# First head pair laid out by compute engines in a written order, expert matrices loaded in pieces, value products and sums placed by tables

## The chip, the core and the metric

One core of a Trainium2 chip runs the program. The metric is the time of one execution on the device in microseconds. Three runs of the kernel before gave 1154.0, 1154.58 and 1159.22 us; their median is 1154.58 us.

## What is computed

Three blocks follow each other. The first is attention over 4 batches of 8 heads (1152 keys of 64 numbers) whose queries are pooled by two; the second sends its output through four causal experts of which each token takes two; the third mixes tokens by two low-rank matrices and ends in an MLP.

```python
# attention: q, k, v are 4 x 8 x 1152 x 64
q_pool = q.reshape(B, H, S // 2, 2, D).mean(axis=3)
scores = scale * np.matmul(q_pool, k.transpose(0, 1, 3, 2))
scores = scores - np.max(scores, axis=-1, keepdims=True)
attn = np.exp(scores)
attn = attn / (np.sum(attn, axis=-1, keepdims=True) + 1e-09)
x = np.matmul(attn, v)              # to 4 x 576 x 512
# experts: per expert q, k, v = x @ wq[e], x @ wk[e], x @ wv[e]; causal softmax,
# @ wo[e], times the token's weight for this expert if it is one of its best two
# tokens and MLP
u = x + (x.transpose(0, 2, 1) @ U @ V).transpose(0, 2, 1)
out = u + np.maximum(u @ w_ch1, 0.0) @ w_ch2
```

## The kernel before

**Pairs and units.** The 32 heads are worked through as 16 pairs. `prep(i)` makes pair `i` ready, `unit(i, u)` is one of its 18 units: a half `h` of the 576 queries against one of nine key tiles `kt`. A unit has two scores (`score(0)` and `score(1)`, one for each head of the pair, in the score tile `st`), the exponentials of them on ACT into `pt`, a running sum of these on POOL (`acc`), and the products with the values (`pv`, two matmuls of half the columns each). After the ninth unit of a half come `post_a` (column sums on TensorE), `post_r` and `post_b` (reciprocal and scaling on DVE). A score is the sum of two matmuls, `q1`·`s1` (line 576) and `q2`·`s2` (line 577): numbers are kept as a high and a low part in fp32r, and one row of `q2` holds minus the maximum of each query's scores.

**What a pair needs first.** `pool_q` adds neighbouring queries into `qp` on DVE (line 495). `tr_q` transposes them on TensorE (511), ACT takes the high part `qh` out of PSUM (517), DVE the low part `ql` (520), and two DMAs for each `tr_q` lay `qh` as blocks into `BD` (522). `tr_k` does the same with the keys: `kn` (361) and `klo` (364). `lay` issues 12 DMAs that copy `qh`, `ql`, `kn` and `klo` into the tiles `q1a`, `q2a`, `s1a`, `s2a` and their twins `q1b` to `s2b`, whose other half of the partitions POOL has filled with constants (351 to 354). The maximum of each query is found by 27 matmuls `mxs` of `BD` with `kn` (543), each reduced by DVE (545) out of one of three PSUM buffers `ms`. `fin` turns the maxima into a row (406, `nm` 408) and sends it by DMA into `q2a` and `q2b` (411); it is called for a block of five and a block of four query tiles, for the first and the second half of the queries.

**Order.** In the attention stage TensorE, DVE and ACT run in the order in which the code is written. `attend` counts two steps for each unit, 36 for a pair. In each step it calls one score, then what `side` holds for that step; tables (`Q_AT`, `K_AT`, `M_AT`, ...) give the steps of `prep(i)` relative to the first step of pair `i`. After every third unit come the value products of three units, the last of which is the unit before the last one scored; `post_a` follows one such group after the half's last product. Pair 0 is prepared ahead of this, by `run_all`, in an order that the scheduler may change, and so are those steps of pair 1 that lie before step 0.

**Loads.** All DMAs are issued by SP in one queue. `expert_weights` loads the expert matrices `wq`, `wk`, `wv`, `wo` and the token matrices U and V one after the other into two halves of a staging tile `stg` (280 to 324), all DMAs of a matrix in one step, and cuts each into a high and a low part, three pieces for a pair of heads (`WC_AT`). U and V are 64-bit numbers, which six DVE instructions turn into 32 bits (248 to 253).

Of the kernel before, what the change touches and what calls it, by code (L numbers as in the profile page):

```python
# [19 lines left out]
GROUP = 3  # L20
POOL_AT, LQ_AT, LK_AT, V_AT = -13, -48, -24, 6
Q_AT = [-7, -1]
K_AT = [-1, 5, 11]
LAY_AT = 13
M_AT = [3, 4, 6, 7, 8, 9, 10, 12, 13, 14, 15, 16, 18, 19, 20, 21, 22, 24, 25, 26, 27, 30, 31, 32, 33, 36, 37]
F_AT = [23, 41]

WL_AT, WC_AT = 20, [17, 23, 35]
# [28 lines left out]
def attend(units, side):  # L57

    n, done, ended, later = len(units), 0, [], {}

    def run(t):
# [5 lines left out]
    def sums(t):  # L69
        nonlocal ended  # L70
        for x in ended:
            x[0]()
            later.setdefault(t + 1, []).append(x[1])
            later.setdefault(t + 4, []).append(x[2])
        ended = []

    for u in range(n):
        for a in range(2):
            units[u][0](a)
            run(2 * u + a)  # L80
        if u % GROUP == GROUP - 1 or u == n - 1:
            last = n if u == n - 1 else u - 1
            sums(2 * u + 1)
            for x in units[done:last]:
                x[1]()
                if x[2]:
                    ended.append(x[2])
            done = last
    sums(2 * n - 1)
    t = 2 * n  # L90
    while side or later:
        run(t)
        t += 1
# [39 lines left out]
def kernel(  # L133
# [36 lines left out]
    nc.vector.tensor_copy(identb, ident)  # L170
    negid = cst.tile([P, 64], F32, name="negid")
    for r in (0, 64):
        nc.vector.tensor_scalar(negid[r:r + 64], ident[r:r + 64, r:r + 64], -1.0, None, op0=ALU.mult)
# [13 lines left out]
    nc.vector.tensor_copy(mask_t, mtmp)  # L187
# [7 lines left out]
    nc.vector.tensor_copy(mask_m[:, T - 64:], mtmp2)  # L195
# [60 lines left out]
    def expert_weights():  # L256
# [17 lines left out]
        def heads(x, w, dst):  # L274
            t = part(x, NC, dst[0].shape[-1])

            def load():
                nc.vector.memset(t[:1, 0, ::HD], 0.0)
                for e in range(E):
                    nc.sync.dma_start(t[:, :, e * HD:(e + 1) * HD], w[e].rearrange("(c p) d -> p c d", p=P))  # L280
                if t.shape[-1] > EW:
                    nc.sync.dma_start(t[:, :, EW:], w_gate.rearrange("(c p) e -> p c e", p=P))

            return load, pieces(t, *dst, 4)
# [638 lines left out]
    with tc.manual_schedule(engines=by_hand):  # L923
        attend(units, side)
# [215 lines left out]
```

## Time and profile before

| | us |
|---|---|
| median of three runs | 1154.58 |
| span of the profiled execution | 1150.9 |
| TensorE busy in it | 1112.5 |
| DVE, POOL, ACT busy | 753.4, 496.2, 459.2 |
| its attention stage | about 32 to 498 |

The span goes from the first to the last instruction; the 3.7 us between it and the median are not in the profile. A matmul's end is modelled, so where matmuls follow each other the distance of their starts tells more than their length. A time in brackets behind a row is idle time of that engine just before it, with what ended it.

### The profile page before, as it was taken

How to read it: one execution, taken by the hardware profiler on the slowest of the kernel's cores; microseconds unless marked ns; L12 is line 12 of the kernel's file. 1: busy time of each engine (PE TensorE's matmuls, PEld its weight loads, DVE VectorE, ACT ScalarE, POOL GpSimd, SP SyncE). 2: the span in 40 equal slices, each digit the busy share in tenths (PEclk: the TensorE clock that was granted, in tenths of full speed). 3: DMA queues.
4: the chain of work that ended last, by engine and by line, in shares of the span. 5: the costliest groups of instructions: out<-in, count | busy, mean ns of one | idle time of the engine just before them, and what ended most of it. 6: DMA issues, size and time to landing. Idle time of an engine off the chain costs nothing.

```text
span 1150.9 us, 19012 instructions
## 1 busy us (share of the span) xinstructions
PE 1112.5 (97%) x6748; PEld 900.0 (78%) x6748; DVE 753.4 (65%) x1613; ACT 459.2 (40%) x1160; POOL 496.2 (43%) x473
## 2 busy tenths in 40 slices
PE   5999999999999999899999998999999999999998
PEld 3777777777777777678777876688899999999997
DVE  6677888888888777566848489946734661663222
ACT  1555666655555555543444535512211111111111
POOL 4688989888788888764324243200000000000000
PEclk9999999999999999999999999999999999999999
DMA  9788787777777764111213134341110220110111
GB/s 223 163 180 195 163 205 170 171 166 166 175 176 166 165 146 118 32 38 46 53 32 94 25 101 166 112 151 55 56 38 19 60 69 1 55 55 1 56 56 55
DMA packets 116958, 120.02 MB, mean 104 GB/s; under 512 B 71680, under 2 KB 88064, under 8 KB 116864
## 3 DMA queue, kind: packets, MB, share of 16 engines
q1 hardware_dynamic: 116864, 118.82, 41.8%
q8 instruction: 53, 0.87, 0.3%
q14 instruction: 41, 0.34, 0.1%
HBM read 52.65 MB, written 9.44 MB: 54 GB/s over the span
## 4 chain that ended last, share of the span: by engine, by line
PE 83%; DVE 12%; ACT 2%; DMA 1%; POOL 1%; issue 1%; SPq 0%; ACTq 0%; POOLq 0%
PE ms L1046 17%; PE o L1057 17%; PE pv L596 11%; PE ms L692 8%; PE st L576 8%; PE ms L543 6%; PE st L577 6%; PE pv L843 2%; DVE mp L545 2%; PE ms L603 2%; DVE ms L767 1%; PE ms L502 1%; DMA bd<-qh 1%; PE st L818 1%; DVE xl L232 1%
## 5 line engine op out<-in xcount | busy, mean ns | idle before, releaser
L588 POOL TENSOR_TENSOR acc<-acc,pt 128x576 f32<-128x576 f32 x224 | 326.5, 1458 | 61.4 <-ACT pt L578 46.8
L578 ACT ACTIVATE pt<-st 128x288 f32<-128x288 f32 x576 | 219.0, 410 | 185.1 <-PE st L577 157.9
L545 DVE TENSOR_REDUCE mp<-ms 128x1 f32<-128x384 f32 x432 | 213.0, 545 | 56.3 <-PE ms L543 55.7
L1046 PE MATMUL ms<-uh,w 128*128 128x384 f32 x768 | 214.7, 340 | 0.9 <-DVE ul L232 0.7
L1057 PE MATMUL o<-w,hh 128*128 128x512 f32 x576 | 180.9, 395 | 0.0
L1050 DVE SCALAR_TENSOR_TENSOR hl<-ms,hh 128x384 fp32r<-128x384 f32 x96 | 53.5, 557 | 186.9 <-ACT hh L1049 186.5
L543 PE MATMUL ms<-kn,bd 128*128 128x384 f32 x432 | 151.7, 361 | 11.9 <-DMA bd<-qh 9.2
L596 PE MATMUL pv<-pt,vr 128*64 128x288 f32 x1152 | 159.6, 413 | 0.0
L1049 ACT ACTIVATE hh<-ms 128x384 fp32r<-128x384 f32 x96 | 47.2, 492 | 270.9 <-PE ms L1046 270.9
L1046 PEld LDWEIGHTS ms<-uh,w 128*128 128x128 f32 x768 | 140.9, 188 | 6.3 <-DVE ul L232 0.9
L1046 PE MATMUL ms<-ul,w 128*128 128x384 f32 x384 | 129.9, 338 | 0.7 <-DVE ul L232 0.7
L1057 PEld LDWEIGHTS o<-w,hh 128*128 128x128 f32 x576 | 107.0, 188 | 17.8 <-issue 0.4
L596 PEld LDWEIGHTS pv<-pt,vr 128*64 128x64 f32 x1152 | 77.1, 137 | 55.5 <-issue 11.2
L1057 PE MATMUL o<-w,hl 128*128 128x512 f32 x288 | 113.6, 394 | 0.0
L543 PEld LDWEIGHTS ms<-kn,bd 128*128 128x128 f32 x432 | 84.0, 195 | 18.6 <-DVE mp L545 7.0
L576 PE MATMUL st<-q1a,s1a 128*128 128x288 f32 x288 | 97.4, 338 | 0.7 <-ACT pt L578 0.7
L576 PEld LDWEIGHTS st<-q1a,s1a 128*128 128x128 f32 x288 | 54.3, 189 | 45.7 <-issue 40.7
L576 PE MATMUL st<-q1b,s1b 128*128 128x288 f32 x288 | 86.2, 299 | 0.4 <-ACT pt L578 0.3
L577 PE MATMUL st<-q2a,s2a 128*128 128x288 f32 x288 | 85.2, 296 | 0.0
L577 PE MATMUL st<-q2b,s2b 128*128 128x288 f32 x288 | 85.0, 295 | 0.0
L1046 PEld LDWEIGHTS ms<-ul,w 128*128 128x128 f32 x384 | 72.2, 188 | 5.1 <-DVE ul L232 1.7
L835 POOL TENSOR_TENSOR acc<-acc,pt 128x576 f32<-128x576 f32 (+4 forms) x48 | 45.4, 945 | 67.1 <-ACT pt L826 65.8
(172 smaller groups left out, 1834.1 us busy)
## 6 DMA issues: line engine op xcount, KB each, us to landing
raw<-in_moe_w_ch_dram SPq DMA_DIRECT2D x32, 512.0 KB
qr<-in_q_dram SPq DMA_DIRECT2D x16, 576.0 KB
vr<-in_v_dram SPq DMA_DIRECT2D x16, 576.0 KB
s1a<-kn SPq DMA_DIRECT2D x32, 288.0 KB
s1b<-kn SPq DMA_DIRECT2D x32, 288.0 KB
kr<-in_k_dram SPq DMA_DIRECT2D x30, 288.0 KB
s2a<-klo SPq DMA_DIRECT2D x16, 288.0 KB
s2b<-klo SPq DMA_DIRECT2D x16, 288.0 KB
```

Of the source, the lines that this page charges most:

```text
L543: nc.tensor.matmul(ps[:, :384], BD[i % 2][:, t, :], KN[i % 2][:, c * 384:c * 384 + 384], start=True, stop=True)
L545: nc.vector.tensor_reduce(st["mp"][:, t, c:c + 1], ps[:, :384], axis=X, op=ALU.max)
L576: nc.tensor.matmul(ps[:, :HT], pr.S1[a][:, ks], pr.Q1[a][:, qs], start=True, stop=False)
L577: nc.tensor.matmul(ps[:, :HT], pr.S2[a][:, ks], pr.Q2[a][:, qs], start=False, stop=True)
L578: nc.scalar.activation(c["pt"][:, a, :], ps[:, :HT], AF.Exp, scale=0.0625)
L588: nc.gpsimd.tensor_add(acc[i, h], acc[i, h], c["pt"])
L596: nc.tensor.matmul(o[64 * a:64 * a + 64, :HT], vr[:, a, kt, :], c["pt"][:, a, :], start=(kt == 0), stop=(kt == NKT - 1))
L692: nc.tensor.matmul(ps, stat[x][s], mov[x][m], start=(x == 0 and y == 0), stop=(x == n - 1 and y == 2))
L1046: nc.tensor.matmul(ps[:, :TB], W[fi][:, 0, a, cs], m[:, c, :], start=(c == 0 and y == 0), stop=(c == NC - 1 and y == 2))
L1049: nc.scalar.activation(h, ps[:, :TB], AF.Relu)
L1050: nc.vector.scalar_tensor_tensor(l, ps[:, :TB], 0.0, f(h), op0=ALU.max, op1=ALU.subtract)
L1057: nc.tensor.matmul(o[s_], hl[m][:, r], W[fi][:, 1, a, :], start=(fi % FG == 0 and y == 0), stop=(fi % FG == FG - 1 and y == 2))
```

## The change

**Pair 0.** `P0` and `P1` are lists in the order of the source. Pair 0 is now prepared inside a manual schedule that covers SP too, so that the four engines keep the written order. Its transposed queries go to a PSUM buffer of the value products; out of it DVE (for the first `tr_q`) and ACT (for the second) write the blocks of `BD` themselves, where four DMAs did. In place of the 12 DMAs of `lay`, `first_q` and `first_k` have ACT write the halves of `q1`, `q2` and `s1` that lie on the same partitions as their source, `first_s` has POOL write `s2`, and one DMA for each of `q1a`, `q1b`, `s1a`, `s1b` carries the half that changes partitions. Loads of pair 1 and of the values come behind these. The second block's twelve `mxs` and its `fin` get steps of their own, `FIRST_AT`; those with a step from 0 on go into `side`, the others are mixed with pair 1's steps, which follow `SECOND_AT`. Four constants are made by ACT instead of DVE.

**Attention order.** `PV_AT` gives the step of each unit's value products, `POST_AT` the steps of `post_a`, `post_r` and `post_b`.

**Expert matrices.** A loader returns a list, one DMA for each expert (two halves for `wo`), and each is placed at its own step, `WD_AT`, from pair 1 of the steps on. Cuts get four steps for a pair. The six DVE instructions for U are six steps (three before), those for V twelve of half the width (six before).

```diff
+FIRST_AT = [-20, -13, -12, -11, -11, -9, -7, -6, -6, -3, -2, 5, 15]
+SECOND_AT = [-15, -10, -6, -2, 4, 8, 19, 6, 7, 7, 9, 10, ... 42, 42, 32, 47]
+PV_AT = [5, 5, 11, 11, 11, 17, 17, 17, 23, 23, 23, 29, 29, 29, 35, 35, 35, 41]
+POST_AT = [[29, 30, 33], [47, 48, 51]]
-WL_AT, WC_AT = 20, [17, 23, 35]
+WL_AT = 10
+WC_AT = [5, 17, 23, 35]
+WD_AT = [15, 18, 21, 24]
...
-def attend(units, side):
+def attend(units, side, period):
+    per = period // 2
+    n, later, vals, ends = len(units), {}, {}, {}
+    for u, (_, pv, post) in enumerate(units):
+        w, x = u // per * period, u % per
+        vals.setdefault(w + PV_AT[x], []).append(pv)
+        if post:
+            for t, g in zip(POST_AT[x * 2 // per], post):
+                (ends if g is post[0] else later).setdefault(w + t, []).append(g)
+    t = 0
+    while t < 2 * n or vals or ends or side or later:
+        if t < 2 * n:
+            units[t // 2][0](t % 2)
...
-    nc.vector.tensor_copy(identb, ident)
+    nc.scalar.activation(identb, ident, AF.Copy)
...
-            def load():
-                nc.vector.memset(t[:1, 0, ::HD], 0.0)
-                for e in range(E):
-                    nc.sync.dma_start(t[:, :, e * HD:(e + 1) * HD], w[e].rearrange("(c p) d -> p c d", p=P))
+            def load(e):
+                nc.vector.memset(t[:1, 0, e * HD:e * HD + 1], 0.0)
+                nc.sync.dma_start(t[:, :, e * HD:(e + 1) * HD], w[e].rearrange("(c p) d -> p c d", p=P))
...
+            for x in (slice(0, HT), slice(HT, T)):
+                if wide:
+                    steps += decode_steps(t[:, x], part(1, T)[:, x].bitcast(I32),
+                                          part(1, T, off=T)[:, x].bitcast(I32), nc.vector)[0]
...
+            if i == 0:
+                for a in range(2):
+                    dst = BD[0][HALF[a], sl.start // 64:sl.stop // 64, HALF[a]]
+                    src = ps[HALF[a], :n].rearrange("p (t j) -> p t j", j=64)
+                    if j0 == 0:
+                        nc.vector.tensor_scalar(dst, src, 1.0, None, op0=ALU.mult)
+                    else:
+                        nc.scalar.activation(dst, src, AF.Copy)
...
+    def first_q(i):
+        for a in range(2):
+            nc.sync.dma_start(f(prs[i].Q1[a][HALF[1 - a]]), f(QHL[1][HALF[a]]))
+            for x in (prs[i].Q1[a], prs[i].Q2[a]):
+                nc.scalar.activation(x[HALF[a]], f(QHL[0][HALF[a]]), AF.Copy)
+
+    def first_k(i):
+        for a in range(2):
+            nc.sync.dma_start(f(prs[i].S1[a][HALF[1 - a]]), f(KN[i][HALF[a]]))
+            nc.scalar.activation(prs[i].S1[a][HALF[a], :S], f(KN[i][HALF[a]]), AF.Copy)
+
+    def first_s(i):
+        for a in range(2):
+            nc.gpsimd.tensor_copy(prs[i].S2[a][HALF[a], :S], f(klo[HALF[a]]))
...
+    with tc.manual_schedule(engines=by_hand | {mybir.EngineType.SP}):
+        P0[0]()
+        low = [P0[1](), P0[2](), P0[3](), P0[4]()]
+        each(low[:2])
+        first_q(0)
+        load_q(1)
+        each(P0[7:9])
+        low.append(P0[5]())
+        first_k(0)
+        load_k(1)
...
+        load_v(0)
+        run_all(sorted([x for x in late + P1 if x[0] < 0], key=lambda x: x[0]))
```

**Where instructions move: TensorE at the start.** `kn_139` and `bd_135` are pair 0's, `kn_140` and `bd_136` pair 1's. Before:

```order
L511 MATMUL ms<-ident,qp 128x96 x6
L502 MATMUL st<-ident,kr 128x128 x9
L543 MATMUL ms<-kn_139,bd_135 128x384 x17
L406 MATMUL ms<-ident,mx 5x128
L543 MATMUL ms<-kn_139,bd_135 128x384 x10
L576 MATMUL st<-q1a_145,s1a_141 128x288
```

And now:

```order
L504 MATMUL pv<-ident,qp 128x96 x6
L495 MATMUL st<-ident,kr 128x128 x6
L547 MATMUL ms<-kn_139,bd_135 128x384 x2
L495 MATMUL st<-ident,kr 128x128 x3
L547 MATMUL ms<-kn_139,bd_135 128x384 x13
L595 MATMUL st<-q1a_145,s1a_141 128x288
L399 MATMUL ms<-ident,mx 5x128
L547 MATMUL ms<-kn_139,bd_135 128x384 x5
```

All 27 `mxs` of pair 0 stood before its first complete score; now 15 do, and the other 12 stand between later ones. From the middle of pair 1 on, TensorE's instructions stand in the same order as before, up to the last value products of the stage.

**DVE at the start.** Before, from the first pooled queries on:

```order
L495 TENSOR_TENSOR qp<-qr 96x2x6x64
L170 CAST identb<-ident 128x128
L173 TENSOR_SCALAR negid<-ident 64x64 x2
L187 CAST mask_t<-mtmp 128x128
L195 CAST mask_m<-mtmp_80 128x64
L495 TENSOR_TENSOR qp<-qr 96x2x6x64
L520 TENSOR_TENSOR ql<-ms,qh 128x384
```

And now:

```order
L488 TENSOR_TENSOR qp<-qr 96x2x6x64
L516 TENSOR_SCALAR bd_135<-pv 64x6x64 x2
L522 TENSOR_TENSOR ql<-pv,qh 128x384
L522 TENSOR_TENSOR ql<-pv,qh 128x192
L549 TENSOR_REDUCE mp<-ms 128x1 x10
L357 TENSOR_TENSOR klo<-st,kn_139 128x384 x2
```

The constants and pair 1's pooling stood between `qp` and `ql`; the writes of `BD` stand there now, and the first `klo` comes behind ten reductions.

**SP in the steps of pair 1.** The rows before hold the loads for pair 2 (tiles 145, 147, ...) and `wk` (`wq` stood seven rows ahead):

```order
L280 DMA stg<-in_moe_wk_dram 128x4x64 x4
L478 DMA kr<-in_k_dram 128x9x64 x2
L532 DMA q1b_146<-qh 64x576
L533 DMA q1b_146<-ql 64x576
L534 DMA q2b_148<-qh 64x576
L373 DMA s1a_141<-kn_139 64x1152 x2
```

Now, from the last DMA of `lay` for pair 2:

```order
L367 DMA s2b_144<-klo 64x1152
L270 DMA stg<-in_moe_wq_dram 128x4x64 x3
L404 DMA q2a_147<-nm 1x5x64
L404 DMA q2b_148<-nm 1x5x64
L270 DMA stg<-in_moe_wq_dram 128x4x64
L462 DMA qr<-in_q_dram 96x2x768
L526 DMA bd_136<-qh 64x6x64 x2
```

Two matrices stood ahead of the key copies of `lay`; one stands behind them, ahead of the next pair's `BD`, and `wk` has moved to the steps of pair 2.

## Rows read from the trace of the kernel before

**Rows 1.** The page: busy time, share of the span and instructions of each engine.
```profile
PE 1112.5 (97%) x6748; PEld 900.0 (78%) x6748; DVE 753.4 (65%) x1613; ACT 459.2 (40%) x1160; POOL 496.2 (43%) x473
```

**Rows 2.** Timeline of TensorE, 0 to 60: start, length, line, idle time before, releaser.
```profile
15.91 8.05 PE L543 MATMUL ms<-kn,bd 128*128 128x384 f32 x17 [6.18 <-DMA bd<-qh]
...
34.66 0.66 PE L543 MATMUL ms<-kn,bd 128*128 128x384 f32 x1 [1.44 <-DMA bd<-qh]
...
37.16 1.01 PE L596 MATMUL pv<-pt,vr 128*64 128x288 f32 x4
```

**Rows 3.** Chain of waits, 0 to 80: start, length, DMAs from issue to release.
```profile
8.83 6.94 DMA bd<-qh
...
31.52 3.00 DMA bd<-qh
```

**Rows 4.** Timeline of SP, 0 to 60: what stood ahead of the blocks.
```profile
6.87 0.97 SPq L485 DMA_DIRECT2D vr<-in_v_dram  x2
8.08 2.84 SPq L522 DMA_DIRECT2D bd<-qh  x4
```

**Rows 5.** Timeline of ACT, 0 to 60.
```profile
7.52 0.71 ACT L517 ACTIVATE qh<-ms 128x384 fp32r<-128x384 f32 x2 [5.50 <-PE ms L511]
8.48 1.13 ACT L361 ACTIVATE kn<-st 128x384 fp32r<-128x384 f32 x2 [0.25 <-PE st L502]
```

**Rows 6.** Timeline of DVE, 0 to 60.
```profile
12.62 0.81 DVE L520 TENSOR_TENSOR ql<-ms,qh 128x384 fp32r<-128x384 f32 x2
13.35 1.47 DVE L364 TENSOR_TENSOR klo<-st,kn 128x384 fp32r<-128x384 f32 x3
16.61 7.54 DVE L545 TENSOR_REDUCE mp<-ms 128x1 f32<-128x384 f32 x16 [1.78 <-PE ms L543]
```

**Rows 7.** Groups by shape on DVE, ACT, POOL: count, busy us, mean ns, idle before.
```profile
L383 DVE TENSOR_TENSOR q1b<-ms,q1b 64x320 fp32r<-64x320 f32 x1 | 0.5, 492 | 0.0
...
L517 ACT ACTIVATE qh<-ms 128x192 fp32r<-128x192 f32 x14 | 4.7, 336 | 0.0
...
L231 ACT ACTIVATE xh<-xt 128x576 fp32r<-128x576 f32 x4 | 2.8, 689 | 0.0
...
L385 POOL CAST bdb<-q1b 64x320 fp32r<-64x320 f32 x1 | 0.5, 453 | 0.1
```

**Rows 8.** What TensorE waited for, 0 to 600: us, times, longest.
```profile
PE ms L543 <- DMA bd<-qh: 9.2, 3, 6.2
...
PE ms L543 <- DVE mp L545: 2.6, 4, 0.9
```

**Rows 9.** Timeline of SP, 60 to 96: expert loads and the next blocks.
```profile
63.19 2.05 SPq L280 DMA_DIRECT2D stg<-in_moe_wq_dram  x4
...
69.27 2.52 SPq L280 DMA_DIRECT2D stg<-in_moe_wk_dram  x4
...
87.38 2.75 SPq L522 DMA_DIRECT2D bd<-qh  x4
```

**Rows 10.** Timeline of TensorE, 86 to 96.
```profile
92.52 0.41 PE L543 MATMUL ms<-kn,bd 128*128 128x384 f32 x1 [1.58 <-DMA bd<-qh]
```

**Rows 11.** Timeline of DVE, 246 to 254.
```profile
249.16 0.86 DVE L248 TENSOR_SCALAR stg<-stg 128x160 int32<-128x160 int32 x1
250.05 1.46 DVE L249 TENSOR_SCALAR stg<-stg 128x160 f32<-128x160 f32 x1
251.43 0.94 DVE L495 TENSOR_TENSOR qp<-qr 96x768 f32<-96x768 f32 x1
```

**Rows 12.** Groups on DVE, 35 to 465: an addition to nine numbers a partition.
```profile
L430 DVE TENSOR_SCALAR d<-d 128x9 f32<-128x9 f32 x29 | 29.0, 1001 | 1.0
```

**Rows 13.** Timeline of all engines, 44.9 to 45.6: exponentials and a value group.
```profile
44.61 1.29 ACT L578 ACTIVATE pt<-st 128x288 f32<-128x288 f32 x3
...
45.38 0.46 PE L596 MATMUL pv<-pt,vr 128*64 128x288 f32 x2
```

**Rows 14.** Timeline of POOL, 0 to 60: its last fill of the pairs' tiles.
```profile
14.03 1.05 POOL L354 MEMSET s2b<- 1x1152 f32 x1
```

More of the change, by code (lines that the diff above doesn't have):

```diff
@@ L67, in run @@
                 later.setdefault(t + 1, []).append(x)
[L69 to L92, printed above, removed]
+        for g in ends.pop(t, []) + vals.pop(t, []):
+            g()
         t += 1
@@ L312, in end @@
                 nc.scalar.activation(MU[:, :, 3 * R:], v_, AF.Copy)
-            return load, [lambda x=x: each(steps[x:x + 2]) for x in range(0, len(steps), 2)] + \
+            return [load], steps + \
                 [lambda: cut(v_, MU[:, :, :R], MU[:, :, R:2 * R], nc.gpsimd), end]
@@ L330, in end @@
                 nc.gpsimd.tensor_sub(MV[r], v_[r], f(MV[r]))
-            return load, steps + [end]
+            return [load], steps + [end]
         return [((0,), *heads(0, wq, (WQK[0][:, 0], WQK[1][:, 0]))),
@@ L513, in tr_q @@
             if j0 == 0:
-                st["q"] = [per_r.tile([P, T], F32R, name=nm) for nm in ("qh", "ql")]
+                st["q"] = QHL[:] = [per_r.tile([P, T], F32R, name=nm) for nm in ("qh", "ql")]
             qh, ql = st["q"]
@@ L517, in tr_q @@
             nc.scalar.activation(qh[:, sl], ps[:, :n], AF.Copy)
+            if i == 0:
[6 more added lines that the diff above has]
+                        nc.scalar.activation(dst, src, AF.Copy)
+                own.update({(t, 0): 0 for t in range(sl.start // 64, sl.stop // 64)})
             def rest():
                 nc.vector.tensor_sub(ql[:, sl], ps[:, :n], f(qh[:, sl]))
+                if i == 0:
+                    return
                 for a in range(2):
@@ L618 @@
     n = 4 * NKT
-    P0, P1 = (sorted(prep(x), key=lambda y: y[0]) for x in range(2))
-    turns = Q_AT + K_AT + [POOL_AT]
+    by_hand = {mybir.EngineType.PE, mybir.EngineType.DVE, mybir.EngineType.Activation}
+    P0, P1 = ([g for _, g in prep(x)] for x in range(2))
+    P1 = list(zip(SECOND_AT, P1))
+    late = list(zip(FIRST_AT, P0[22:34] + [P0[35]]))
+    place(side, [x for x in late if x[0] >= 0], 0)
     load_q(0)
     load_k(0)
-    run_all([x for x in P0 if x[0] in turns])
-    load_k(1)
-    load_q(1)
-    load_v(0)
-    run_all([x for x in P0 if x[0] not in turns and x[0] < F_AT[1]])
-    run_all([x for x in P1 if x[0] < 0])
-    run_all([x for x in P0 if x[0] == F_AT[1]])
+    with tc.manual_schedule(engines=by_hand | {mybir.EngineType.SP}):
[8 more added lines that the diff above has]
+        load_k(1)
+        each(P0[9:17])
+        each(low[2:4])
+        each(P0[17:19])
+        each(low[4:])
+        first_s(0)
+        each(P0[19:22] + [P0[34]])
+        load_v(0)
+        run_all(sorted([x for x in late + P1 if x[0] < 0], key=lambda x: x[0]))
     slots = [x + n * w for w in range(2, NP - 2) for x in WC_AT]
     free = [n + 2, n + 10]
-    for halves, load, steps in expert_weights():
+    queue = [x + n * w for w in range(1, NP - 2) for x in WD_AT]
+    for halves, loads, steps in expert_weights():
         at = max(free[h] for h in halves) + 1
-        place(side, [(at, load)], 0)
+        for g in loads:
+            while queue[0] < at:
+                queue.pop(0)
+            at = queue.pop(0)
+            place(side, [(at, g)], 0)
         while slots[0] < at + WL_AT:
```

33 lines of the change are left out of this document (16 added, 17 removed).

## The prediction

> **What bounds the kernel now.** I read the page's busy times first. TensorE is busy for 1112.5 of 1150.9 us [rows 1], so the change can gain only where TensorE waits: 38.4 us by this count, and what a wait hides inside a matmul's modelled end. The change does not shorten any matmul. Next came TensorE's timeline at the start, to see which wait ends last there. Two lie in it: 6.18 us before the first `mxs`, and 1.44 us before pair 1's first [rows 2]. The chain of waits names the releaser of both, a DMA that lays `qh` into `BD`: 6.94 us from issue to release for pair 0, 3.00 us for pair 1 [rows 3]. SP's timeline says why the first took over twice as long: it was issued behind two loads of values [rows 4]. Then I asked what TensorE waited for over the whole attention stage. Three waits on these DMAs sum to 9.2 us and four on DVE's reductions to 2.6 [rows 8]; the third DMA wait, 1.58 us, stands at 92.52 [rows 10], and SP's timeline shows 4.57 us of expert loads and then a late issue of the blocks ahead of it [rows 9]. Between these stretches TensorE's matmuls follow each other without a break, and nothing that speeds up another engine there can show.
>
> **The start, term by term.** I take as a yardstick the first group of value products, at 37.16 us [rows 2].
> - ACT takes the first high part out of PSUM at 7.52 and is done with both at 8.23 [rows 5]; nothing ahead of this changes, since the four constants that move to ACT can run in the 5.50 us for which ACT was idle there. DVE's writes of `BD` go behind the first of these evictions, from about 8.0. They are PSUM reads of 64x384; the nearest row is 64x320 in 0.49 [rows 7], so 0.55 each, done at 9.1. ACT writes its two of 64x192 meanwhile (0.34 each, by the 128x192 row of [rows 7]) and the first `kn` (two took 1.13 [rows 5]), done at about 9.4. The first `mxs` can start at 9.5, where it stood at 15.91: 6.4 us.
> - From 9.1 DVE sets the pace. Ahead of the first value group it has two `ql` (0.81 [rows 6]), 26 reductions of 7.54 / 16 = 0.47 (12.2), three `klo` (1.47), pair 1's pooling (0.94 [rows 11]), two more `ql` (0.81) and a small maximum (0.2): 16.4 us, ending at 25.5, and 0.2 for the first matmul's end. The 27th `mxs` and the last exponential follow: value products at 26.4 instead of 37.16, 10.8 us earlier. The gain exceeds the 6.4 because scores now run beside pair 0's last 12 reductions, where they waited for all 27.
> - At that point the kernel before had two `mxs` of pair 1 done, which are now still to come: 0.4 for both (one took 0.41 with its tail [rows 10], and tails overlap). The start is worth **10.4**.
> - Cover that this needs: the row of maxima has to be in `q2a` when TensorE comes to the second matmul of the first score, at about 22.5. The 15th reduction ends at about 18.7; transpose, eviction and SP's issue take it to 19.8; with the 3.00 of [rows 3] it lands at 22.8. The key copies (ACT: 0.69 for 128x576 [rows 7], so some 1.4 for each 64x1152) and their DMAs are done by then, and POOL's two `s2` are 1152 / 320 of 0.45 at most [rows 7], 1.6 each, from 17 on. All of it ends within a microsecond of the need; if the load of pair 1's keys, issued just ahead, delays it as the values delayed the blocks (6.94), the row lands at 26.7 and the value products slip to about 30. So the term lies between **6.8 and 10.8**.
>
> **The rest of pairs 0 and 1.** Twelve steps took 45.38 - 37.16 = 8.2 us [rows 2, 13], 0.7 each. Two rows of maxima are now called late: pair 0's second at step 15 for a score at step 18, pair 1's first at step 32 for step 36. The first leaves 2.1 us and a bit, against 0.5 to the issue and 3.00; the second leaves 2.8 and SP has the twelve DMAs of `lay` (from step 19) ahead of it. I take 0.5 and 0.6 off: **-1.1**, with 0 and -4 as ends, the latter if each waits for a load as long as the 3.9 by which 6.94 exceeds 3.00, less what is covered. Neither wait shows in the trace of before, where both rows came earlier.
>
> **Expert loads.** 4.57 us of SP's time, two matrices, leave the stretch ahead of pair 2's blocks; one matrix comes back behind `lay`, about 2.1 [rows 9]. The blocks were issued at 87.38 and needed 1.58 us earlier than they landed; issued 2.4 earlier they are in time: **+1.6**, between 0 and 1.6. The other matrices were loaded without such a wait and are spread further; nothing for them.
>
> **U and V on DVE.** Where decoding meets the next pair's pooling, DVE holds TensorE up: 0.86 + 1.46 + 0.94 in a row at 249 [rows 11]; four such waits make the 2.6 of [rows 8]. Single steps and half widths cut the row roughly by half, but twelve halves take more steps and meet the pooling about as often: **+1.3**, between -1.5 and 2.6. A rule of the Trainium skill speaks against the halves. First the row: an addition to nine numbers a partition takes 1001 ns in the mean [rows 12], longer than the 0.47 of a reduction over 384. The skill's page "SBUF — State Buffer", section "SBUF: two separate sides", says that VectorE and GpSimd share a pair of ports under an exclusive lock that is held for a whole instruction, and that the loser blocks; POOL adds all through this stage, so twelve instructions can be held up where there were six. The row agrees with that; it does not say that TensorE feels it.
>
> **Value products one unit earlier.** The same number of groups at the same steps, each with its last unit nearer to its exponentials. At 44.61 ACT begins three exponentials of 0.43; the value group starts at 45.38 [rows 13]. The first of the three, ended at 45.04, is the last that the group will now need, and its products stand at the end of the group. Cost nothing, covered by 0.3 us and the group's first eight matmuls.
>
> **The sum.** 10.4 - 1.1 + 1.6 + 1.3 = 12.2 off the profiled execution's 1150.9: 1138.7. The median stands 3.7 above that span (1154.58), so **1142.4**. With the favourable ends 10.8 + 0 + 1.6 + 2.6 = 15.0, 1139.6; a granted clock that fell after the pause before 34.66, where one `mxs` took 0.66 against 0.41 at 92.52 [rows 2, 10], may give another microsecond, 1138.5. With the unfavourable ends 6.8 - 4 + 0 - 1.5 = 1.3, 1153.3, which wants all of them at once.
>
> **Rivals.**
> - The new path waits for its loads. For it: rows of maxima, values and pair 1's keys all share SP's queue, and every margin at the start is about a microsecond. Against it: four DMAs now do what sixteen did there. The start then gives 6.8 and pairs 0 and 1 lose 2.5: 1154.6 - 6.8 + 2.5 - 1.6 - 1.3 = 1147.4. Chance 0.17.
> - The later waits only move. For it: DVE is the busiest after TensorE, and the lock of the shared ports would make twelve halves of V cost 6 x 1.0 us more of DVE. By the skill's lock alone, if TensorE felt half of that, U and V would come to -1.5. With nothing from the expert loads either: 10.4 - 1.1 - 1.5 = 7.8, 1146.8. Against it: DVE idles a third of the time. Chance 0.12.
> - Slower: value products wait for ACT. There are six groups in each of 16 pairs, 96. If ACT runs one exponential further behind than at 44.61, each group would stand for up to 0.43: 41 us, 1184. It decides from 12.2 / 96 = 0.13 us a group. Against it: the cover above. Chance 0.04.
> - The change does not do what it says: the engines' writes of pair 0's tiles wait for POOL, which fills all the constants first, and the DMAs' time comes back as that wait. POOL fills the last constant tile of the pairs from 14.03 to 15.08 [rows 14], just before the old first `mxs`; with only 1.6 + 1.3 left, 1151.7. Against it: the writes wait for their own tile only, and `BD` is filled first. Chance 0.05.
>
> **How the numbers follow.** The forecast has 0.62. Its own spread is 1138.5 to 1145; the first two rivals reach to 1149; the last two, 0.09, stay out, with a part of the tails. A measurement of this kernel tells 0.5% from no change, 5.8 us: faster is below 1148.8. That takes in the forecast, most of the first rival and nearly all of the second: 0.85. The same: 0.11. Slower: 0.04.
>
> **What would show each step.** TensorE's first `mxs` at 9.5 and first value group near 26.4, with DVE nearly without idle time between 10 and 26. A wait in front of the first matmul on `q2a` (line 596 of the changed kernel) at 22 to 24, at step 18 or at pair 1's first score would be the first rival. No wait for `BD` by a DMA after the start. Waits on DVE's reductions of at most half of 2.6 us between 200 and 360. In the timeline of a value group, no idle time ahead of or inside it. The prediction is wrong if the first value group comes after 31, or if it comes near 26 and the attention stage still ends less than 8 us earlier.

## The result and the profile after

The changed kernel took **1142.77 us** in the median of four runs (1142.18 to 1143.29); the kernel before took 1155.92 beside it. The ratio is 0.9878, with a 95% interval from 0.9855 to 0.9900: faster by 1.2%. The profiled execution has a span of 1141.5 us, 9.4 below that of before. Its page answers to [rows 1]:

```profile
PE 1109.1 (97%) x6748; PEld 900.2 (79%) x6748; DVE 739.5 (65%) x1625; ACT 464.6 (41%) x1173; POOL 499.6 (44%) x475
```

TensorE is busy 3.4 us less than before and waits 6.0 us less (1141.5 - 1109.1 = 32.4 against 38.4). The timeline of TensorE at the start, for [rows 2] (start, length, line, idle time before, releaser):

```profile
9.44 0.98 PE L547 MATMUL ms<-kn,bd 128*128 128x384 f32 x2 [0.32 <-ACT kn L354]
...
19.20 0.38 PE L399 MATMUL ms<-ident,mx 128*5 128x128 f32 x1 [0.60 <-DVE mx L552]
...
21.88 0.69 PE L547 MATMUL ms<-kn,bd 128*128 128x384 f32 x1 [0.64 <-DVE mp L549]
...
23.76 0.44 PE L596 MATMUL st<-q2a,s2a 128*128 128x288 f32 x1
...
28.26 1.19 PE L615 MATMUL pv<-pt,vr 128*64 128x288 f32 x8
...
53.07 0.40 PE L595 MATMUL st<-q1a,s1a 128*128 128x288 f32 x1
56.03 0.40 PE L596 MATMUL st<-q2a,s2a 128*128 128x288 f32 x1 [2.56 <-DMA bd<-qh]
```

The first `mxs` comes at 9.44 (15.91 before), the first score finds its row of maxima in place at 23.76, and the first value group starts at 28.26 (37.16 before). Then, at 53, TensorE stands for 2.56 us in front of pair 1's first `q2a` matmul. A table by stretch shows what the clock did (columns: stretch, length, busy time and count of PE, PEld, DVE, ACT and POOL, then the granted clock, the DMA share and GB/s):

```profile
10.00:15.00 5.00, 4.72 (x15) 2.70 (x13) 4.74 (x11) 4.91 (x7) 4.95 (x7) 1.00 0.72 181
15.00:20.00 5.00, 3.43 (x8) 1.69 (x8) 4.17 (x11) 0.27 (x2) 2.29 (x2) 0.54 1.18 211
20.00:25.00 5.00, 4.36 (x14) 2.90 (x13) 4.41 (x9) 0.90 (x2) 0.00 (x0) 0.50 0.50 135
25.00:30.00 5.00, 5.00 (x34) 3.97 (x34) 4.16 (x10) 2.87 (x9) 2.55 (x2) 0.94 0.52 103
...
55.00:60.00 5.00, 3.97 (x18) 3.78 (x18) 1.12 (x2) 2.47 (x6) 1.41 (x1) 0.66 0.70 160
...
759.00:764.00 5.00, 5.00 (x19) 4.64 (x18) 1.23 (x4) 0.49 (x1) 0.00 (x0) 0.66 0.00 0
```

TensorE is at its lower level, 1.2 GHz, from 15 to 25, for part of 55 to 60 and for part of 759 to 764. A 1.00 ahead of the first fall does not tell the level: in e6, below, scores start 0.24 us apart under a printed 1.00 up to 31.2, as they do at 0.50 here, and 0.13 apart from 31.5 on.

To see where time goes or comes from I compare the two kernels at the matmuls that add up a half pair (line 603 before, 622 after), 32 places that both pass in the same order. At the eighth, the rows of before and of after are

```profile
154.84 0.71 PE L603 MATMUL ms<-acc,ones 128*64 128x288 f32 x4
```
```profile
150.06 0.71 PE L622 MATMUL ms<-acc,ones 128*64 128x288 f32 x4
```

and 154.84 - 150.06 = 4.78 is the **lead** of the changed kernel there. The table gives the lead of every kernel of this study at six of these places, named by their time in the kernel before, and how much it grows from 98.67 to 467.10.

| kernel | median us | ratio to before (95%) | 54.18 | 68.77 | 98.67 | 239.29 | 356.56 | 467.10 | growth |
|---|---|---|---|---|---|---|---|---|---|
| changed | 1142.77 | 0.9878 (0.9855, 0.9900) | 8.1 | 2.8 | 4.4 | 5.5 | 10.7 | 11.2 | 6.7 |
| e10, changed again | 1144.69 | 0.9895 (0.9875, 0.9915) | 7.6 | 2.2 | 4.2 | 5.2 | 10.3 | 10.7 | 6.6 |
| e1, row early | 1142.21 | 0.9890 (0.9871, 0.9908) | 7.9 | 3.6 | 5.6 | 6.6 | 11.8 | 12.2 | 6.7 |
| e2, blocks by DMA | 1144.11 | 0.9907 (0.9889, 0.9925) | 4.8 | -0.1 | 1.9 | 2.9 | 8.1 | 8.5 | 6.6 |
| e3, decode in pairs | 1144.82 | 0.9911 (0.9895, 0.9927) | 7.0 | 3.3 | 5.3 | 5.3 | 9.5 | 10.6 | 5.3 |
| e4, loads whole | 1144.71 | 0.9912 (0.9895, 0.9928) | 7.6 | 1.9 | 3.9 | 3.4 | 8.1 | 8.5 | 4.7 |
| e5, all rows early | 1141.26 | 0.9869 (0.9848, 0.9890) | 6.7 | 5.5 | 7.0 | 7.7 | 12.9 | 13.3 | 6.3 |
| e6, loads ahead | 1145.01 | 0.9911 (0.9896, 0.9926) | 1.5 | 0.0 | 1.8 | 2.8 | 8.0 | 8.4 | 6.6 |
| e7, decode as before | 1146.29 | 0.9921 (0.9906, 0.9936) | 7.4 | 1.2 | 3.2 | 4.3 | 6.3 | 6.4 | 3.2 |
| e8, values later | 1141.03 | 0.9876 (0.9861, 0.9891) | 8.8 | 3.5 | 5.5 | 6.6 | 11.8 | 12.3 | 6.8 |
| e9, sums behind | 1145.69 | 0.9911 (0.9891, 0.9931) | 6.7 | 2.8 | 4.1 | 4.2 | 8.5 | 8.1 | 4.0 |
| e12, sums and decode | 1148.60 | 0.9925 (0.9899, 0.9951) | 6.9 | 0.8 | 2.8 | 3.0 | 4.0 | 3.3 | 0.5 |
| e11, rows early, values later | 1139.72 | 0.9855 (0.9833, 0.9876) | 7.3 | 5.9 | 7.9 | 9.0 | 14.1 | 14.5 | 6.6 |

e1 to e4, e5 to e8 and e9 to e12 ran on one chip each, beside the kernel before (medians 1155.02, 1155.40 and 1156.12). The first line tells the story: the lead is 8.1 at 54, and 5.2 of it are lost before 69. It wins 1.6 back before 99, 1.1 to 239 and 5.2 to 357, and reaches 11.2 at 467. A median is rough here (the changed kernel gave 1142.77 and 1144.69), while the growth column repeats within 0.5 us in kernels whose code is the same in that stretch: 6.3 to 6.8 in eight of them. The two traces of the changed kernel give 6.74 and 6.58, and their mean, 6.66, is the base for what the others lose.

Each lead comes from one trace, and the medians alone would judge some theories otherwise. Against 1142.77, from another chip, e1 is 0.6 us faster and e5 1.5, both inside what their rivals B allowed, and e2 is only 1.3 slower. Against 1144.69, from the same chip, e9 is 1.0 slower where theory A wanted 2 to 4, and e12 3.9 where it wanted about 5.

### The profile page after: what moved, and what is told of

It is laid out like the page before. It is cut to its first block, busy times and chain, and to the rows that moved or that the text cites. A ratio compares the mean times of both kernels' runs of the same rounds, so it can differ in the third digit from the quotient of the medians.

```text
span 1141.5 us, 19024 instructions
## 1 busy us (share of the span) xinstructions
PE 1109.1 (97%) x6748; PEld 900.2 (79%) x6748; DVE 739.5 (65%) x1625; ACT 464.6 (41%) x1173; POOL 499.6 (44%) x475
## 3 DMA queue, kind: packets, MB, share of 16 engines
HBM read 52.65 MB, written 9.44 MB: 54 GB/s over the span
## 4 chain that ended last, share of the span: by engine, by line
PE 85%; DVE 10%; ACT 2%; POOL 1%; issue 1%; DMA 1%; SPq 0%; ACTq 0%; POOLq 0%
PE ms L1083 17%; PE o L1094 17%; PE pv L615 12%; PE ms L730 8%; PE st L595 8%; PE ms L547 6%; PE st L596 6%; PE pv L881 2%; PE ms L622 2%; DVE mp L549 2%; PE ms L495 1%; DVE ms L805 1%; PE st L856 1%; DVE xl L223 1%; POOL acc L607 1%
```

## Experiments: the start and the entry of pair 1

Two things were to be explained: why the start gave less than forecast, and why most of it was gone at 69. In the changed kernel, DVE had the maximum of pair 1's first block at 41.71, and SP issued its row ten microseconds later:

```profile
41.71 0.17 DVE L552 TENSOR_REDUCE mx<-mp 128x5 f32<-128x15 f32 x1
```
```profile
36.27 0.68 SPq L404 DMA_DIRECT2D q2a<-nm  x1
...
37.69 0.54 SPq L536 DMA_DIRECT2D q1a<-qh  x1
...
43.58 2.85 SPq L366 DMA_DIRECT2D s1b<-kn  x2
46.47 1.34 SPq L367 DMA_DIRECT2D s2b<-klo  x1
47.91 1.34 SPq L462 DMA_DIRECT2D qr<-in_q_dram  x1
49.35 1.88 SPq L526 DMA_DIRECT2D bd<-qh  x2
51.34 0.76 SPq L404 DMA_DIRECT2D q2a<-nm  x1
```

From 36.27 to 51.34 SP issues 17 DMAs without a pause: pair 0's second row, the twelve of pair 1's `lay`, a load of queries and two blocks.

**e1, the row alone earlier.** Pair 1's first `fin` at step 24 in place of 32. (Steps of `prep(i)` count from the first step of pair `i - 1`: the code places them at `(i - 1) * n`. So these count from the start of pair 0.)

```diff
-SECOND_AT = [..., 42, 42, 32, 47]
+SECOND_AT = [..., 42, 42, 24, 47]
```

> The changed kernel with one number changed: pair 1's first row of maxima is called at step 24 and not 32. In the changed kernel this row's maximum was ready on DVE at 41.71, its DMAs were issued at 51.34, behind a load of queries and two blocks, and TensorE stood for 2.6 us before pair 1's first q2a matmul, then ran at a granted clock of 0.66 until 60. Theory A (the late call is what holds TensorE): the row's DMAs are issued right behind the last DMA of lay, at about 47.9, and land by 51.5; no wait at 53 and no fall of the clock; 4.5 us faster than the changed kernel (3.0 to 5.2), about 1138.3. Rival B (the DMA engines are full there, so the row lands when it lands, or the wait is for the blocks, as the trace's releaser says): the wait stays at 2 us or more and the time within 1 us of 1142.8.

The row is issued at 47.90, as theory A said, and the wait at 53 is gone. But TensorE now stands a few scores later, for the blocks of pair 2, which went behind the row on SP:

```profile
56.29 0.63 PE L547 MATMUL ms<-kn,bd 128*128 128x384 f32 x1 [1.40 <-DMA bd<-qh]
```

The clock fell there too. The lead at 467 is 1.1 above the changed kernel's, not the 4.5 of theory A: the late call is a cause, but behind it stands the whole late row of issues.

**e5, the whole row earlier.** Three numbers: pair 0's second `fin`, pair 1's `lay` and its first `fin`.

```diff
-FIRST_AT = [..., -3, -2, 5, 15]
+FIRST_AT = [..., -3, -2, 5, 7]
-SECOND_AT = [-15, -10, -6, -2, 4, 8, 19, ..., 42, 42, 32, 47]
+SECOND_AT = [-15, -10, -6, -2, 4, 8, 11, ..., 42, 42, 24, 47]
```

> The changed kernel with three numbers changed: pair 0's second row of maxima at step 7 and not 15, pair 1's lay at 11 and not 19, its first row at 24 and not 32. With the row alone at 24, TensorE's wait of 2.6 us at pair 1's first score became one of 1.4 us on pair 2's blocks, since SP's issues from 36.3 to 53.8 stand in one unbroken row. Theory A (the lateness of the whole row of issues is what costs): the row starts some 4 us earlier, no wait of over 0.3 us between 50 and 66, the clock stays at 1.00 there, and the lead over the kernel before that stood at 8.1 us at 46 stays: about 5 us faster than the changed kernel (4 to 6), 1137.8. Rival B (the transfers fill the DMA engines there, and the wait goes somewhere else): a wait of over 1 us remains between 35 and 66; within 2 us of the changed kernel, 1141 to 1143.

SP's row starts at 32.01 instead of 36.27; TensorE has no wait over 0.12 us between 50 and 66, and the clock stays up there:

```profile
50.00:55.00 5.00, 5.00 (x37) 3.77 (x36) 3.69 (x8) 3.15 (x9) 3.64 (x4) 1.00 0.79 167
55.00:60.00 5.00, 4.96 (x35) 3.67 (x33) 1.98 (x4) 3.04 (x8) 3.80 (x3) 1.00 0.63 136
...
460.00:470.00 10.00, 8.08 (x47) 6.86 (x44) 6.14 (x7) 3.28 (x9) 4.48 (x3) 0.83 0.11 26
```

Between 54 and 69 it loses 1.1 us, not 5.2. That is theory A's mechanism, but the gain at 467 is 2.2 us and not 4 to 6: this execution was 1.4 us behind the changed kernel at 54 already, of it 1.05 at the first value group (29.31) with the same code up to there. Its granted clock was 0.68 from 25 to 30, against 0.94 in the changed kernel. And the clock fell once more at 460 to 480, where it lost another 1.4.

**e2, the blocks by DMA.** Pair 0's `BD` laid by four DMAs again, with the loads still behind.

```diff
-            if i == 0:
-                for a in range(2):
-                    dst = BD[0][HALF[a], ...]
-                    ...
             def rest():
                 nc.vector.tensor_sub(ql[:, sl], ps[:, :n], f(qh[:, sl]))
-                if i == 0:
-                    return
                 for a in range(2):
                     nc.sync.dma_start(f(BD[i % 2][HALF[a], ...
```

> The changed kernel, but pair 0's blocks are laid into BD by four DMAs again, as in the kernel before; its loads stay behind them and everything else of the new start stays. Theory A (the start gained by two halves: the engines' writes, and the loads that no longer stand ahead): the DMAs take about 3.0 us each as pair 1's did before, not 6.94, so the first mxs comes at about 12.5 instead of 9.44 and the kernel is 3 us slower than the changed one (2 to 4), about 1145.8. Rival B (the engines' writes are the whole gain): the first mxs comes at about 15.9 as before, 6.4 us slower, 1149.2. Rival C (DVE's reductions set the pace however the blocks come, and a late first mxs is caught up): within 1 us of 1142.8.

```profile
11.69 0.98 PE L536 MATMUL ms<-kn,bd 128*128 128x384 f32 x2 [2.40 <-DMA bd<-qh]
```

2.25 us later than with the engines' writes, and 2.7 less lead at 467: theory A by the lead, at the lower end of its 2 to 4, though the medians differ by less.

**e6, the loads ahead as well.**

```diff
+        load_q(1)
+        load_v(0)
         each(low[:2])
         first_q(0)
-        load_q(1)
```

(and without the `load_v(0)` that stood behind.)

> The changed kernel with pair 0's blocks by DMA again and, ahead of them on SP, pair 1's load of queries and two loads of values, as in the kernel before. The same without the loads ahead had its first mxs at 11.69 (9.44 in the changed kernel) and lost 2.65 us by the end of the attention stage. Theory A (the loads ahead were the larger half of the old wait): the first mxs comes at 15 to 16, and another 3 to 4 us are lost, about 1149. Rival B (the loads don't matter, since the DMAs of the blocks share the engines with the loads in any order): the first mxs comes within 1 us of 11.69, time about 1145.

```profile
15.71 0.98 PE L536 MATMUL ms<-kn,bd 128*128 128x384 f32 x2 [6.61 <-DMA bd<-qh]
...
60.69 0.37 PE L585 MATMUL st<-q2b,s2b 128*128 128x288 f32 x1 [0.35 <-DMA q2b<-nm]
```

Of the first `mxs` theory A is right: 15.71, the old 15.91 within 0.2 us. So the start gains 6.3 us at this place, 2.25 by the engines' writes and 4.0 by the order of the loads. The time is B's, 1145.01, for a reason that neither theory has: the lead, 1.5 at 54, loses only 1.5 before 69, where the changed kernel loses 5.2. After the later start TensorE comes to pair 1 when the rows are there. The changed kernel's 6.6 us more at 54 are 2.9 us more at 69: **over half of what the start gained was lost again at the entry of pair 1.**

**e10, the changed kernel again.**

> The changed kernel unchanged, as the measure for the others on the same chip. Theory A (what moved the earlier runs by up to 3 us is where the granted clock falls, at the start, at pair 1's first score and where the stages join, and not the change): 1141 to 1145, first mxs at 9.4, the wait at pair 1's first score at 2.3 to 3.4 us. Rival B (the wait at pair 1 was an accident of the first trace): no wait of over 1 us there.

```profile
PE st L596 <- DMA q2a<-nm: 2.7, 1, 2.7
```

The wait is no accident: 2.7 us here, and 2.3 to 3.4 in the others that have this code. Here the list of waits names the row of maxima itself as the releaser, where the first trace named a block.

## Experiments: from 94 to 467

**e8, values later.** `PV_AT` as in the kernel before.

```diff
-PV_AT = [5, 5, 11, 11, 11, 17, 17, 17, 23, 23, 23, 29, 29, 29, 35, 35, 35, 41]
+PV_AT = [5, 11, 11, 11, 17, 17, 17, 23, 23, 23, 29, 29, 29, 35, 35, 35, 41, 41]
```

> The changed kernel with the value products at the steps of the kernel before (one unit later in each group). Theory A (the shift costs and gains nothing in itself): the leads at all half pairs within 0.5 us of the changed kernel's, time within 1 us of 1142.8. Rival B (the shift sets the phase between DVE's small operations and POOL's additions: the 128x9 addition took 1051 ns in the mean before and 530 after): that mean goes back above 900, and between 94 and 346 us one to three microseconds are lost.

The growth is 6.8 against 6.7 and the mean of the 128x9 addition 531 ns: no effect in the steady part, as theory A says. The lead is above the changed kernel's all along, by 0.7 us at 54 already and by 1.1 from 99 on. The changed kernel's own second trace, e10, lies 0.3 to 0.7 below its first, so the 0.5 us of the expectation was too narrow.

**e3 and e7, the decoding.** e3 undoes the widths; e7 undoes the fourth slot as well.

```diff
-            return [load], steps + \
+            return [load], [lambda x=x: each(steps[x:x + 2]) for x in range(0, len(steps), 2)] + \
...
-            for x in (slice(0, HT), slice(HT, T)):
-                ...
+            steps, v_ = decode_steps(t, part(1, T).bitcast(I32), ...
```
```diff
-WC_AT = [5, 17, 23, 35]
+WC_AT = [17, 23, 35]
```

> The changed kernel with the decoding of U and V as it was in the kernel before: U two steps at a time, V over its full width in six steps; the slots (5, 17, 23, 35) stay the new ones. Between 233 and 346 us the changed kernel gained 5.2 us on the kernel before. Theory A (the gain is that no two decoding steps stand in a row ahead of the pooling): TensorE's waits on DVE's reductions come back in this stretch, 2.5 us or more, and the kernel is 4 us slower (2.5 to 5.2), about 1146.8. Rival B (the gain is the new slots, or DVE's waits for POOL, and not the widths): the stretch stays within 1 us and the time within 1 us of 1142.8.

> The changed kernel with the decoding of U and V as before in both respects: double steps of U, whole width of V, and the slots 17, 23, 35 without 5. With the widths alone undone the lead over the kernel before grew by 4.0 us between 234 and 386 us all the same, where the changed kernel's grew by 5.1. Theory A (the fourth slot takes most decoding steps away from the pooling at step 23): most of the rest is lost too, waits on DVE's reductions of 2.5 us or more come back and the lead at 450 us is 2.5 to 5 us smaller than the changed kernel's 11.2. Rival B (the rest comes from the phase between DVE and POOL, which the decoding doesn't set): the lead at 450 stays within 2 us of the changed kernel's, as with the widths alone (0.5 smaller).

What TensorE waited for between 200 and 400 us (us, times, longest), in the changed kernel, e3 and e7; the kernel before had 2.6 there in four waits [rows 8]:

```profile
PE ms L547 <- DVE mp L549: 0.5, 1, 0.5
```
```profile
PE ms L544 <- DVE mp L546: 1.1, 2, 0.6
```
```profile
PE ms L544 <- DVE mp L546: 2.7, 4, 0.8
```

With the widths alone undone the growth falls by 1.3 (6.66 to 5.34), less than theory A of e3 wanted. With the slots too it falls by 3.4 (to 3.22) and the four waits are back: theory A of e7. So the decoding is worth 3.4 us, and with the widths already undone the fourth slot is 2.1 of it; no run undoes the slot alone.

**e9, the sums behind.** With the decoding undone there are still 3.2 us of growth (e7), which no term of the prediction explains. The timelines of DVE and POOL around one half pair's sums, first before, then after, show a moved order:

```profile
155.47 0.56 DVE L364 TENSOR_TENSOR klo<-ms,kn 128x384 fp32r<-128x384 f32 x1 [0.47 <-ACT kn L361]
155.94 0.47 DVE L428 STREAM_TRANSPOSE d<-ms 128x288 f32<-128x288 f32 x1
156.45 1.37 DVE L430 TENSOR_SCALAR d<-d 128x9 f32<-128x9 f32 x1
```
```profile
153.40 4.40 POOL L588 TENSOR_TENSOR acc<-acc,pt 128x576 f32<-128x576 f32 x3 [0.85 <-ACT pt L578]
```
```profile
150.81 0.48 DVE L421 STREAM_TRANSPOSE d<-ms 128x288 f32<-128x288 f32 x1 [0.59 <-PE ms L622]
151.33 0.23 DVE L423 TENSOR_SCALAR d<-d 128x9 f32<-128x9 f32 x1
...
151.73 0.50 DVE L357 TENSOR_TENSOR klo<-ms,kn 128x384 fp32r<-128x384 f32 x1
```
```profile
148.62 4.41 POOL L607 TENSOR_TENSOR acc<-acc,pt 128x576 f32<-128x576 f32 x3
```

Before, `klo` stands ahead of the transpose; after, behind. Nine numbers a partition take 1.37 us before because POOL's third addition ends only at 157.80, and 0.23 after because its second ends at 151.54. The copy of the reciprocals follows on ACT, at 158.11 before, and the next exponentials behind it at 158.46. The change has the order from its tables: `attend` enters the reciprocals into `later` before the loop starts, and a low part is appended when its first half has run. e9 restores the old order alone:

```diff
-                (ends if g is post[0] else later).setdefault(w + t, []).append(g)
+                (ends if g is post[0] else mids if g is post[1] else later).setdefault(w + t, []).append(g)
...
-        for g in later.pop(t, []) + side.pop(t, []):
+        for g in later.pop(t, []) + mids.pop(t, []) + side.pop(t, []):
```

> The changed kernel with one order undone: where a step holds both the reciprocal of a half pair's sums and a low part of keys or queries, DVE takes the low part first, as in the kernel before (the new tables put the sums first, 26 times between 90 and 450 us). Theory A (this order is a gain that was not forecast: DVE's 128x9 addition waits for the end of a POOL addition, and coming 0.5 us earlier it meets an earlier end, so that ACT's copy behind it no longer delays the exponentials): the mean of the 128x9 addition goes from 530 back to 900 ns or more, and the lead over the kernel before stops growing between 94 and 234 us (it grew by 1.1) and grows by 1.5 to 2 less between 234 and 346: 3 us slower in all (2 to 4). Rival B (DVE has idle time for it, and the phase against POOL comes from elsewhere): mean below 700 ns, leads within 0.5 us.

The groups of this addition in 90 to 450 us, of before, the changed kernel and e9 (count, busy us, mean ns, idle before):

```profile
L430 DVE TENSOR_SCALAR d<-d 128x9 f32<-128x9 f32 x25 | 26.6, 1063 | 0.9
```
```profile
L423 DVE TENSOR_SCALAR d<-d 128x9 f32<-128x9 f32 x26 | 13.8, 530 | 0.9
```
```profile
L423 DVE TENSOR_SCALAR d<-d 128x9 f32<-128x9 f32 x26 | 24.3, 934 | 0.9
```

The mean is back, the lead stands still from 99 to 239 (4.1 to 4.2), and the growth is 4.0: 2.6 less than the changed kernel's. By the leads theory A holds, with a smaller share than expected between 239 and 357 (0.9) and a larger one behind it.

TensorE's list of waits shows none of this: 0.5 us between 99 and 467 in the changed kernel, and 0.5 in e9. The starts of its matmuls do. Between 99 and 467 the starts of e9 fall behind those of e10 by two steps of some 0.1 us at one place in each pair, 13 times; no other step is over 0.08. It is the score behind the copy of the reciprocals, where the low part is one of keys; where it is one of queries nothing is lost. The same place before, and after:

```profile
158.62 0.36 PE L543 MATMUL ms<-kn,bd 128*128 128x384 f32 x1
158.90 0.40 PE L576 MATMUL st<-q1a,s1a 128*128 128x288 f32 x1
159.14 0.30 PE L577 MATMUL st<-q2a,s2a 128*128 128x288 f32 x1
```
```profile
153.83 0.34 PE L547 MATMUL ms<-kn,bd 128*128 128x384 f32 x1
154.01 0.29 PE L595 MATMUL st<-q1a,s1a 128*128 128x288 f32 x1
154.14 0.29 PE L596 MATMUL st<-q2a,s2a 128*128 128x288 f32 x1
```

The starts are 0.28 and 0.24 us apart before, 0.18 and 0.13 after: 0.2 us in a pair, and 13 x 0.2 is 2.6. No row has idle time there, since the matmuls' modelled ends cover it.

**e12, both undone.**

> The changed kernel with both undone: DVE's low parts ahead of the sums, and the decoding of U and V with the widths and slots of the kernel before. Theory A (these two are the whole gain between 94 and 360 us): the lead grows by no more than 1 us from 94 to 360, where the changed kernel's grew by 5.9 (4.42 to 10.36); about 5 us slower than the changed kernel. Rival B (something else in the tables, as the value products one unit earlier, has a part): the lead grows by 2 us or more.

The lead grows by 0.4 us from 99 to 370 (it stands 1.3 up at 357 and loses that again at a wait behind it) and by 0.5 to 467. The two parts add up: 2.62 + 3.44 = 6.06 of 6.66, and undoing both takes 6.1.

**e4, the loads whole.** All DMAs of an expert matrix at one step; the decoding steps stay.

```diff
-        for g in loads:
+        place(side, [(at, g) for g in loads], 0)
+        for g in loads:
             while queue[0] < at:
                 queue.pop(0)
             at = queue.pop(0)
-            place(side, [(at, g)], 0)
```

> The changed kernel, but all DMAs of one expert matrix are called at one step again, the step that the kernel before would have used (for the first two matrices steps 39 and 47); the steps of the work on them stay as changed. Theory A (the whole loads held pair 2's blocks up): a wait for a DMA of about 1.6 us returns near 88 us in front of pair 2's first mxs, and the kernel is 1.6 us slower (1.0 to 2.2), about 1144.4. Rival B (the wait of 92.52 came from pair 1's own order on SP, not from the loads): no wait there, within 0.6 us of 1142.8.

First a correction of names: with the pairs counted from 0, as the code does, SP issues four blocks at 30.79 for pair 1, at 55.17 for pair 2 and at 87.38 for pair 3, so what the prediction and the expectation here call pair 2's blocks are pair 3's. No wait returns near 88; the lead grows by 2.0 from 69 to 99, as in the other kernels (1.3 to 2.0). So far rival B. But a wait for blocks stands at another pair,

```profile
145.66 0.41 PE L547 MATMUL ms<-kn,bd 128*128 128x384 f32 x1 [0.93 <-DMA bd<-qh]
```

and the growth is 4.7, 2.0 less than the changed kernel's. The pieces pay, at another place than forecast. What took the wait of [rows 10] away is not settled: it is 0.5 us or less in all twelve kernels, and in none was the rest of SP's order there put back.

**e11, early rows and later values**, the tables of e5 and e8 together.

> The kernel with pair 0's second row at step 7, pair 1's lay at 11 and its first row at 24, and with the value products at the steps of the kernel before. Theory A (the early rows are worth 2.2 us by the end of the attention stage, the value products nothing): a lead of 13 to 14 us at 455 us, no wait of over 0.5 us between 50 and 66, and a time 2 us below the changed kernel's on the same chip (1 to 3). Rival B (a clock that falls elsewhere takes it back, as at the join in the first trace of the early rows): the lead at 455 is the same, the time within 1 us of the changed kernel's.

1139.72 against 1144.69 for the changed kernel on the same chip, by more than theory A asked; 0.9855 of the kernel before, where e5 and e8 were 0.9869 and 0.9876. The lead is 14.5 at 467 (it fell by 1.5 right behind it, where the clock fell as in e5). By e8 the later values have no part in this, so the early rows bring the 3.8 us of lead (5.9 against 2.2 at 69, 14.5 against 10.7 at 467). Of these 3.8 the fall of the clock leaves 2.2 at the end of the two traces; that the medians differ by as much as 5.0 is not explained.

## Why the prediction was right in its number, and wrong in its shares

Forecast 1142.4, measured 1142.77, inside the range. The sum was 12.2 us off the span and 9.4 came; the median stood 1.3 above the changed kernel's span, not 3.7, and these 2.4 us covered most of the difference. That is luck: in the changed kernel's runs a time is 1.8 above its own span, in runs of the kernel before 1.7 to 2.8, so the rest of 3.7 and of 1.3 says only which execution was profiled. The shares were far off, in both directions:

| term | forecast | measured, and by what |
|---|---|---|
| start | +10.8 at the first value group, +10.4 in all | +8.9 at the first value group, +8.1 at 54 |
| rest of pairs 0 and 1 | -1.1 | -5.2 (lead from 54 to 69) |
| expert loads, the blocks at 87.38 | +1.6 | +1.6 (69 to 99), cause not shown |
| decoding of U and V | +1.3 | +3.4 (e7) |
| value products | 0 | 0 (e8) |
| order of DVE's sums | not seen | +2.6 (e9) |
| rest of the growth, 99 to 467 | - | +0.6 |
| behind 467 | 0 | -1.8, of it 1.5 where the clock was low at 759 |

- **The start.** The first `mxs` was right to 0.1 us (9.5, 9.44). The step that failed is "from 9.1 DVE sets the pace": it added up DVE's busy time and forecast the first value group at 26.4. DVE was idle for 2.2 us between 10 and 28. The two longest cases are round trips: TensorE had stood for DVE (0.60 and 0.64 above) before it made what DVE took next, and at its lower clock:

```profile
19.94 0.56 DVE L549 TENSOR_REDUCE mp<-ms 128x1 f32<-128x384 f32 x1 [0.79 <-PE ms L547]
...
23.81 0.56 DVE L522 TENSOR_TENSOR ql<-ms,qh 128x384 fp32r<-128x384 f32 x1 [0.59 <-ACT qh L510]
```

  Up to the 15th reduction the count holds (it ends at 18.94, worked out 18.7); the 1.9 us are lost behind it. From 22.36 to the value group at 28.26 TensorE has no idle time in its rows, so there it sets the pace and not DVE, and up to 25.6 it does so at 1.2 GHz. What that costs can be read from kernels with the same code up to there: the first value group stands at 28.06 with a granted clock of 0.97 from 25 to 30 (e8), at 28.26 with 0.94, 28.71 with 0.84 (e10), 28.97 with 0.74 (e11), 29.31 with 0.68 (e5) and 29.69 with 0.63 (e9). From 0.97 to 0.63 is 3.4 us more at the lower level and 1.63 us later, 0.48 a microsecond. By this, the 3.2 us from 22.36 to 25.6 cost 1.6 of the missing 1.9: an estimate, as no run had the clock up there.

  Of the cover, the row of maxima was in time, as worked out (issued at 19.96, needed at 23.76).
- **The rest of pairs 0 and 1.** The step that failed is the price, 0.6 for pair 1's row, with -4 as the end for both; 5.2 lies outside that end. The prediction saw the twelve DMAs of `lay` ahead, but did not work out when SP comes to its end: 17 issues from 36.27 took 15.1 us. Moving the start ahead moves TensorE towards this row, since SP's row moves along by less. Against e6, with its late start, TensorE comes to pair 1 6.6 us earlier (53.07, 59.68), and SP to pair 1's row of maxima 5.8 earlier (51.34, 57.13). And from this issue to TensorE's next matmul pass 4.7 us, where e6 has 2.8: the mean DMA share is 1.00 from 51 to 54 here and 0.41 from 57 to 60 there. The first rival has this mechanism ("the new path waits for its loads") with 2.5 us; it was the forecast's own case that needed it, in double size. Pair 0's second row, priced at 0.5, cost nothing: no wait stands between 28 and 53.
- **Expert loads.** The size came true, the reason is doubtful: whole loads do not bring the wait back (e4).
- **Decoding.** Right in sign and place, 2.1 short. The argument weighed widths and said that halves meet the pooling about as often; the fourth slot, which the diff shows as one number, took them away from it.
- **Value products** cost nothing, as worked out.
- **Not seen** was that the tables also turn the order of two DVE operations in 28 places of the attention stage. The step that failed is "nothing that speeds up another engine there can show": it was read from rows without idle time, and 2.6 us lay in the starts. The prediction quoted the 1001 ns of this very addition [rows 12], and read it as a price for the decoding steps, not as something that its own place decides.
- **Rivals.** "The new path waits for its loads" came true at the entry of pair 1, and the early rows show that it need not. "The later waits only move" did not: its twelve halves, held up by POOL, were to make U and V cost 1.5, and U and V gave 3.4. "Value products wait for ACT" did not come: the list of TensorE's waits has no value product. "The change doesn't do what it says" fell with the first `mxs` at 9.44.

## What to carry to other kernels

A gain at the start is worth what the next fixed queue lets through: list when each engine's program, SP's issues too, comes to the thing that TensorE needs next, before the gain is booked. When code turns a call order into tables, compare the order of the small operations too, since a nine-number operation can cost 1.4 us at one place and 0.2 at the next. A list of waits shows only what the rows call idle; a tenth of a microsecond between the starts of matmuls, 26 times, was worth as much as the four waits on DVE of [rows 8]. A forecast that hits the total is checked by leads at matched places; here errors of 6.5 us (start and entry) and 5.4 us (growth) hid each other, by luck.

## What the hardware showed beyond expectation

**DVE's small addition ends when POOL's addition ends.** Between 35 and 470 us, 25 of the 30 such additions of the kernel before, and all 30 of the changed one, began while POOL was adding; each ended 28 to 33 ns after the end of POOL's addition, and the five that met none took 172 to 174 ns. The transposes beside them took 0.47 to 0.48 us throughout. The Trainium skill's page "SBUF — State Buffer", section "SBUF: two separate sides", says that VectorE, in some forms of its instructions, and GpSimd share a port pair under an exclusive lock, held for a whole instruction; these rows agree with that for the small addition, while the transposes are not held up.

**Some issues on SP took longer while the DMA engines were full.** In the row from 36.27 most issues take 0.5 to 0.7 us; two for `s1b`, at 43.58, take 2.85 and one for `s2b` 1.34, where the DMA share was 0.97 to 0.98 from 40 to 50, against 0.36 from 36 to 40. But two for `s1a`, at 41.47, took 0.62 each under the same share, and that the one causes the other was not tried.

**The clock falls at different places in executions of the same code.** After TensorE's pauses near 757 (0.9 and 0.7 us) it stayed at 2.4 GHz in the trace of before and fell in the first trace of the changed kernel, for about 1.5 us of time; in e2, e3, e4, e5, e11 and e12 it fell between 464 and 480, and each lost 1.4 to 1.5 us of lead there. With identical code up to 28 us, the first value group stood between 28.06 and 29.69, the later the longer the clock stayed at its lower level. Two executions of this kernel that differ by less than 2 us tell little by their times alone.
